# Windowed attention and a gated feed-forward on one core: whole loads per batch and kind, stores of 32 or 64 rows, and a new order

## The chip, the cores and the metric

One core of one Trainium2 chip runs the whole program. The metric is the device time of one execution, in microseconds (us); three executions of the kernel before gave 328.67, 329.82 and 332.52 us, median 329.82 us.

## The reference, cut to what matters

Shapes: 8 batches, 8 heads, 576 tokens, 64 features a head; the model width is 512, the hidden width 1024.

```python
mask_plain = (rel >= 0) & (rel < 32)                        # heads 0 to 3
mask_dil   = (rel >= 0) & (rel < 128) & (rel % 4 == 0)      # heads 4 to 7
attn = softmax(where(mask, q @ k.T / 8, -1e9))
x = (attn @ v)                                              # [batch, token, 512]
for b in range(8):
    scores = x[b] @ w_gate                                  # one gate score per token
    top = the 128 tokens of highest score
    ye = relu(x[b, top] @ w1) @ w2
    out[b, top] = x[b, top] + sigmoid(scores[top])[:, None] * ye
```

All other rows of `out` are `x`. All inputs and the output are float32.

## The kernel before, in words

**Attention units.** Each batch is cut into five units `u`. Units 0 and 1 take the dilated heads ("kind 1"), two of the four residues of the token number each; units 2 and 3 take the plain heads ("kind 0"), 256 tokens each; unit 4 takes the last 64 tokens of both kinds. A unit's steps are `scores` (S: 8 mask products L327 and up to 64 score products L335 into the PSUM tile `s`), `maximum` (MX), `subtract` (SU, both VectorE), `turn` (TR, 4 transposes), `exps` (EX, ScalarE), `attend` (V: 64 products with the values L370 into the PSUM tile `a`), `divisors` (DN), `divide` on VectorE (XM, L392) or on ScalarE (XA, L390, eight instructions), `store` (ST). `s` and `a` have one buffer each.

**Loads.** `load_qk` (LQ, L255 to 283) loads what one unit needs of queries and keys into one of four buffers `qk`; `load_v` (LV, L288 to 302) loads a unit's values into one of four buffers `v` (or `vl` for unit 4). Runs are 1024 and 1152 bytes for queries and keys of units 0 to 3, 192 to 384 bytes in unit 4, 2080 or 4160 bytes for values. They take 2560 KB and 2145 KB a batch. All are issued by SyncE (SP), whose instructions run in order, so that a DMA which waits (for a buffer, or for the rows it stores) holds up every one behind it.

**Stores.** `store` (L394 to 408) writes a unit's 128 x 512 tile `x` to the output in runs of 1024 bytes. For units 0 to 3 it issues two DMAs of 128 rows and 128 KB each, one for each half `e` of the tile:

```python
dst = o[0:4*P, 256:512].rearrange("(e n r) f -> e r n f", e=2, r=DIL)      # units 0 and 1
nc.sync.dma_start(out=dst[1 - e, 2*u:2*u + 2], in_=x[:, e])                # outermost size of out: r = 2
dst = o[...].rearrange("(c e q) f -> c q e f", e=2, q=G)                   # units 2 and 3
nc.sync.dma_start(out=dst[:, :, e], in_=x[:, e])                           # outermost size of out: c = 4
```

Unit 4 has three smaller DMAs (L405: 32 rows, L408: 16 rows twice) whose output has an outermost size of 32 and 16.

**Routing and feed-forward.** Gate sums per token: GM and GA (GpSimd, then ScalarE) or GD (VectorE); RO, SC, SP and SB bring them in order of the tokens and make a row of them; RK, RC and RA rank them; MK (GpSimd) and MV (VectorE) mark, one token block an instruction (L490), which token has which rank; PK picks the indices (PE), GT gathers the 128 rows (GpSimd DMA). The weights (LW, 16 DMAs of 256 KB through four buffers `raw`) are split once into two parts (WH or WV, and WL on GpSimd). XT, XH and XL turn and split the gathered rows; N (one batch) or F (a pair of batches) is the first product, Y the second, YO the sum and SY the scatter (GpSimd DMA). Pairs are set by the GROUP lines: 0, 1, (2, 3), (4, 5), (6, 7).

**Order.** The order of all steps over all engines is written out by hand in the string ORDER (L42 to 111); each engine takes its own instructions in that order. Nine idle products on a zero tile (L660) run ahead of it.

Of the kernel before, what the change touches and what calls it, by code (L numbers as in the profile page):

```python
# [8 lines left out]
F32 = mybir.dt.float32  # L9
F32R = mybir.dt.float32r  # L10
BF16 = mybir.dt.bfloat16
# [8 lines left out]
P = 128  # L20
# [8 lines left out]
QW, KW = 256, 288  # L29
LQ, LK = 128, 48  # L30
# [6 lines left out]
BUFS = dict(qk=4, v=4, s=1, dt=2, pt=2, a=1, x=5, gm=2, m=4, xe=4, h=1, raw=4, oh=1, sb=1, rm=1, xh=1, xl=1, hh=1, hl=1, mx=3, den=3, rin=3, rx=2, g=8, ix=8, junka=1, junkv=1)  # L37
# [6 lines left out]
GROUP 1 1  # L44
GROUP 2 2 3
GROUP 3 4 5
GROUP 4 6 7
LQ 0 0, C 1, C 5, LQ 0 1, LW 0, LQ 0 2, LV 0 0, C 6, LQ 0 3, S 0 0, C 2, MX 0 0, SU 0 0, LV 0 1, WH 0, S 0 1, WL 0,
LW 1, C 3, TR 0 0, MX 0 1, LW 2, EX 0 0, SU 0 1, LQ 0 4, V 0 0, S 0 2, DN 0 0, LW 3, XA 0 0, TR 0 1, MX 0 2, LV 0 2,
LW 4, SU 0 2, LQ 1 0, TR 0 2, LV 0 3, WV 1, S 0 3, C 4, EX 0 1, EX 0 2, ST 0 0, V 0 1, MX 0 3, WH 2, SU 0 3, LQ 1 1,  # L50
WH 3, DN 0 1, S 0 4, XM 0 1, LV 0 4, TR 0 3, MX 0 4, GM 0 0, V 0 2, EX 0 3, SU 0 4, ST 0 1, GD 0 1, TR 0 4, WL 3,
LQ 1 2, GA 0 0, S 1 0, LV 1 0, DN 0 2, EX 0 4, WL 1, RX 0, WV 4, XA 0 2, LW 5, MX 1 0, LQ 1 3, WL 2, SU 1 0, TR 1 0,
WL 4, LW 6, S 1 1, ST 0 2, GM 0 2, V 0 3, MX 1 1, LW 7, LW 8, EX 1 0, DN 0 3, XM 0 3, GA 0 2, LV 1 1, SU 1 1, V 0 4,
GM 0 3, ST 0 3, S 1 2, DN 0 4, XM 0 4, LQ 1 4, GA 0 3, TR 1 1, MX 1 2, GM 0 4, V 1 0, EX 1 1, SU 1 2, ST 0 4, DN 1 0,
S 1 3, GA 0 4, WV 5, WL 5, TR 1 2, XA 1 0, MX 1 3, LV 1 2, RO 0, LV 1 3, SU 1 3, LQ 2 0, SC 0, TR 1 3, SP 0, LW 9,
EX 1 2, V 1 1, GM 1 0, ST 1 0, SB 0, DN 1 1, LQ 2 1, EX 1 3, RK 0 0, S 1 4, XA 1 1, RK 0 1, LV 1 4, RK 0 2, LQ 2 2,
# [12 lines left out]
GM 2 4, MV 1 3, TR 3 2, MV 1 4, ST 2 4, V 3 0, GA 2 4, S 3 3, DN 3 0, LV 3 4, XM 3 0, PK 1, EX 3 2, MX 3 3, GM 3 0,
ST 3 0, RO 2, SG 1, SU 3 3, HT 0 1, LQ 4 2, SH 1, GA 3 0, V 3 1, IX 1, SC 2, GT 1, LV 4 0, HI 0 1, S 3 4, DN 3 1,  # L70
LV 4 1, XA 3 1, HO 0 1, TR 3 3, MX 3 4, LQ 4 3, SP 2, Y 0 2, SU 3 4, LV 4 4, Y 0 3, EX 3 3, GD 3 1, V 3 2, SB 2,
ST 3 1, S 4 0, RX 3, DN 3 2, XM 3 2, LV 4 2, TR 3 4, MX 4 0, LQ 4 4, GM 3 2, XT 1, EX 3 4, Y 0 4, SU 4 0, XH 1,
Y 0 5, RK 2 0, GA 3 2, ST 3 2, TR 4 0, RK 2 1, V 3 3, RK 2 2, S 4 1, EX 4 0, LV 4 3, DN 3 3, XM 3 3, Y 0 6, LQ 5 0,
MX 4 1, GM 3 3, Y 0 7, ST 3 3, SU 4 1, V 3 4, RK 2 3, GA 3 3, S 4 2, RK 2 4, LV 5 4, DN 3 4, XL 1, XA 3 4, TR 4 1,
MX 4 2, LQ 5 1, RC 2, N 1 0 0, RA 2, SU 4 2, MK 2 0, N 1 0 1, MV 2 4, MK 2 1, TR 4 2, YO 0, EX 4 1, ST 3 4, MK 2 2,
V 4 0, GD 3 4, MK 2 3, S 5 0, EX 4 2, LV 5 0, SY 0, DN 4 0, PK 2, XM 4 0, LQ 5 2, MX 5 0, RO 3, GM 4 0, SG 2, ST 4 0,
SU 5 0, N 1 0 2, SH 2, TR 5 0, GA 4 0, IX 2, SC 3, GT 2, S 4 3, V 4 1, MX 4 3, LQ 5 3, SP 3, EX 5 0, SU 4 3, LV 5 1,
N 1 0 3, SB 3, DN 4 1, TR 4 3, XA 4 1, RK 3 0, N 1 1 0, N 1 1 1, RK 3 1, N 1 1 2, RK 3 2, N 1 1 3, RK 3 3, RL 1 0,
ST 4 1, GD 4 1, S 4 4, RL 1 1, RK 3 4, V 4 2, LQ 5 4, MX 4 4, RC 3, EX 4 3, SU 4 4, HT 1 0, DN 4 2, HT 1 1, HI 1 0,
RA 3, LV 5 2, TR 4 4, MV 3 0, MK 3 3, XA 4 2, MV 3 1, XT 2, MV 3 2, MK 3 4, S 5 1, RX 4, HO 1 0, PK 3, MX 5 1,  # L80
LQ 6 0, SU 5 1, XH 2, V 4 3, GM 4 2, ST 4 2, SG 3, IX 3, XL 2, HI 1 1, S 5 2, LV 5 3, EX 4 4, GT 3, DN 4 3, TR 5 1,
SH 3, LQ 6 1, XA 4 3, MX 5 2, Y 1 0, SU 5 2, Y 1 1, HO 1 1, TR 5 2, Y 1 2, GA 4 2, GM 4 3, ST 4 3, V 4 4, S 5 3,
DN 4 4, EX 5 1, LV 6 4, XM 4 4, GA 4 3, XT 3, MX 5 3, ST 4 4, V 5 0, XH 3, SU 5 3, Y 1 3, EX 5 2, DN 5 0, LQ 6 2,
GD 4 4, XA 5 0, TR 5 3, LV 6 1, Y 1 4, XL 3, RO 4, Y 1 5, SC 4, GD 5 0, ST 5 0, V 5 1, S 5 4, EX 5 3, LV 6 2, DN 5 1,
XM 5 1, SP 4, LQ 6 3, MX 5 4, GM 5 1, Y 1 6, SB 4, ST 5 1, SU 5 4, Y 1 7, RK 4 0, GA 5 1, TR 5 4, V 5 2, RK 4 1,
S 6 0, EX 5 4, LV 6 0, DN 5 2, RK 4 2, XA 5 2, F 2 0 0, LQ 6 4, MX 6 0, F 2 0 1, SU 6 0, F 2 0 2, RK 4 3, RK 4 4,
TR 6 0, RX 5, YO 1, GM 5 2, ST 5 2, V 5 3, S 6 1, DN 5 3, EX 6 0, LV 6 3, SY 1, XA 5 3, RC 4, MX 6 1, LQ 7 0,
F 2 0 3, RA 4, SU 6 1, MK 4 3, F 2 1 0, MV 4 0, MV 4 1, TR 6 1, MV 4 2, GA 5 2, F 2 1 1, ST 5 3, GD 5 3, V 5 4,
HH 2 0, MV 4 4, S 6 2, HL 2 0, EX 6 1, LV 7 4, DN 5 4, PK 4, XM 5 4, LQ 7 1, F 2 1 2, SG 4, MX 6 2, ST 5 4, F 2 1 3,
SU 6 2, F 2 2 0, HH 2 1, GD 5 4, TR 6 2, V 6 0, SH 4, IX 4, HL 2 1, GT 4, S 6 3, EX 6 2, LV 7 0, DN 6 0, RO 5,  # L90
XA 6 0, MX 6 3, LQ 7 2, SU 6 3, F 2 2 1, SC 5, TR 6 3, SP 5, F 2 2 2, GD 6 0, ST 6 0, SB 5, V 6 1, RK 5 0, S 6 4,
EX 6 3, LV 7 1, DN 6 1, F 2 2 3, RK 5 1, LQ 7 3, XA 6 1, MX 6 4, F 2 3 0, SU 6 4, F 2 3 1, RK 5 2, F 2 3 2, HH 2 2,
# [22 lines left out]
def tile_window_attention_moe(ctx, tc, qt, kt, va, vb, w_gate, w1, w2, masks, mask_l, ident, slots, toks, outs, capacity):  # L115
# [647 lines left out]
```

## Time and profile before

| | |
|---|---|
| median of three executions | 329.82 us |
| the profiled execution's own time | 329.4 us |
| its span, first to last instruction | 327.5 us |
| mean granted TensorE clock | 0.84 of full speed |
| PE busy | 247.0 us (75%) |
| VectorE, ScalarE, GpSimd busy | 154.5, 113.9, 94.5 us |
| moved by DMA | 57.86 MB |

How to read it: the engines run beside each other, each in its own order, so their busy times don't add up. The profiled execution lasts 1.9 us longer than its span; that is outside the first and the last instruction. The DMA share is the mean over 16 DMA engines: 0.125 can be two of them always busy or all of them an eighth of the time. Where queues overlap it can pass 1 a little.

### The profile page before, as it was taken

The numbers are of one execution on the slowest core, as the hardware profiler recorded it, in microseconds if no ns is written. First come the engines' busy times: TensorE is split into PE (matmuls) and PEld (weight loads), VectorE is DVE, ScalarE is ACT, GpSimd is POOL, SyncE is SP. The second block draws the span as 40 slices with busy tenths as digits, with TensorE's granted clock in tenths as the row PEclk, the third lists the DMA queues.
The fourth block names the chain that finished last, engine by engine and source line by source line (L and its number), as shares of the span: only waits on it lengthen the run. The fifth ranks groups of instructions, "written<-read, shape, count | busy, mean of one in ns | idle before, by whom it ended". The sixth has DMA issues, their size and how long they took to land.

```text
span 327.5 us, 14421 instructions
## 1 busy us (share of the span) xinstructions
PE 247.0 (75%) x6345; PEld 206.5 (63%) x6345; DVE 154.5 (47%) x437; ACT 113.9 (35%) x383; POOL 94.5 (29%) x122
## 2 busy tenths in 40 slices
PE   5665455376769289772099859879978999999993
PEld 2554345264656178661088748769866889989982
DVE  5346234525458246572027737765944662630310
ACT  1325136333343525240015724434524665200200
POOL 7258023634154122134010501201122454130111
PEclk9555559656599769799559999999979999999998
DMA  6967586776696478676775596557755614101001
GB/s 189 292 157 275 158 268 170 249 228 207 174 275 220 141 217 270 218 212 183 231 237 157 152 298 181 176 159 228 215 177 155 191 67 127 49 20 47 32 7 59
DMA packets 55454, 57.86 MB, mean 177 GB/s; under 512 B 18656, under 2 KB 46432, under 8 KB 55392
## 3 DMA queue, kind: packets, MB, share of 16 engines
q1 hardware_dynamic: 53824, 52.65, 53.7%
q0 software_dynamic: 1280, 4.20, 3.8%
q8 instruction: 50, 0.82, 1.1%
q10 hardware_dynamic: 288, 0.10, 0.1%
q14 instruction: 12, 0.10, 0.1%
HBM read 45.39 MB, written 11.53 MB: 174 GB/s over the span
## 4 chain that ended last, share of the span: by engine, by line
PE 42%; DMA 27%; issue 17%; SPq 7%; POOL 2%; DVE 2%; ACT 1%; POOLq 0%
DMA qk<-in_kt_dram 10%; PE py L617 7%; PE a L370 7%; PE s L335 7%; PE ph L574 6%; DMA out_dram<-x 6%; SPq L264 5%; PE t L354 4%; DMA vl<-in_va_dram 3%; DMA raw<-in_w_dram 3%; PE pi L498 2%; PE ph L591 2%; DMA qk<-in_qt_dram 2%; DMA wg<-in_gate_dram 2%; PE s L327 1%
## 5 line engine op out<-in xcount | busy, mean ns | idle before, releaser
L335 PE MATMUL s<-qk 64*32 64x64 f32 (+1 forms) x2432 | 40.7, 252 | 46.3 <-DMA qk<-in_kt_dram 40.4
L335 PEld LDWEIGHTS s<-qk 64*32 64x32 f32 (+1 forms) x2432 | 33.5, 119 | 50.8 <-DMA qk<-in_kt_dram 21.3
L420 POOL TENSOR_TENSOR gm<-x,wg 128x512 f32<-128x512 f32 x28 | 35.9, 1284 | 83.1 <-DVE x L392 53.7
L341 DVE TENSOR_REDUCE mx<-s 128x8 f32<-128x512 f32 x40 | 27.5, 688 | 63.2 <-PE s L335 63.2
L359 ACT ACTIVATE pt<-t 128x512 f32<-128x512 f32 x40 | 24.0, 600 | 78.6 <-PE a L370 57.2
L370 PE MATMUL a<-v,pt 64*32 64x65 f32 x2048 | 31.5, 248 | 12.4 <-DMA v<-in_va_dram 7.7
L390 ACT ACTIVATE x<-a,rin 128x64 f32<-128x64 f32 x168 | 36.7, 336 | 9.9 <-PE a L370 5.3
L370 PEld LDWEIGHTS a<-v,pt 64*32 64x32 f32 x2048 | 25.2, 116 | 18.9 <-issue 15.1
L354 PE MATMUL t<-id,dt 128*128 128x128 f32 x160 | 31.9, 334 | 2.6 <-DVE dt L346 2.6
L574 PE MATMUL ph<-xh,w1h 128*128 128x256 f32 x96 | 28.2, 294 | 0.1
L346 DVE TENSOR_TENSOR dt<-s,mx 128x512 f32<-128x512 f32 x40 | 27.6, 690 | 1.2
L617 PE MATMUL py<-w2h,hh 128*128 128x512 f32 x64 | 28.1, 440 | 0.0
L354 PEld LDWEIGHTS t<-id,dt 128*128 128x128 f32 x160 | 22.6, 169 | 8.4 <-DVE dt L346 3.0
L574 PE MATMUL ph<-xl,w1h 128*128 128x256 f32 x96 | 27.0, 281 | 0.4 <-issue 0.4
L430 ACT ACTIVATE junk<-gm 128x256 bf16<-128x256 f32 x56 | 23.5, 420 | 10.7 <-POOL gm L420 9.7
L574 PE MATMUL ph<-xh,w1l 128*128 128x256 f32 x96 | 26.9, 281 | 0.0
L380 DVE TENSOR_SCALAR den<-a 128x8 f32<-128x8 f32 x40 | 6.6, 164 | 43.0 <-PE a L370 42.8
L617 PE MATMUL py<-w2l,hh 128*128 128x512 f32 x64 | 26.0, 406 | 0.0
L617 PE MATMUL py<-w2h,hl 128*128 128x512 f32 x64 | 26.0, 406 | 0.0
L470 DVE SCALAR_TENSOR_TENSOR rm<-sb,ts,thr 128x576 bf16<-128x576 f32 (+4 forms) x40 | 23.7, 635 | 2.2 <-ACT sb L462 2.2
L490 POOL TENSOR_SCALAR oh<-slots_sb,rk 128x128 f32<-128x128 f32 (+1 forms) x17 | 11.0, 652 | 40.6 <-DVE rk L484 40.6
L518 POOL DMA_INDIRECT xe<-out_dram,ix x8 | 8.5, 1064 | 42.2 <-DVE ix L502 19.9
(100 smaller groups left out, 415.1 us busy)
## 6 DMA issues: line engine op xcount, KB each, us to landing
v<-in_va_dram SPq DMA_DIRECT2D x16, 520.0 KB
out_dram<-x SPq DMA_DIRECT2D x64, 128.0 KB
qk<-in_qt_dram SPq DMA_DIRECT2D x31, 256.0 KB
qk<-in_kt_dram SPq DMA_DIRECT2D x23, 288.0 KB
v<-in_va_dram SPq DMA_DIRECT2D x16, 260.0 KB
raw<-in_w_dram SPq DMA_DIRECT2D x16, 256.0 KB
qk<-in_kt_dram SPq DMA_DIRECT2D x24, 96.0 KB
v<-in_va_dram SPq DMA_DIRECT2D x16, 130.0 KB
```

Source lines behind the costliest of these rows:

```text
L335: nc.tensor.matmul(st[G * a:G * a + m, h, i * GK + lo:i * GK + hi], q[r, hh, q0:q0 + m], k[r, hh, k0 + lo:k0 + hi], start=False, stop=i == 3)
L341: nc.vector.tensor_reduce(out=mx, in_=st[:, :, 0:4 * GK].rearrange("p u (i k) -> p u i k", i=4), axis=AX.X, op=ALU.max)
L346: nc.vector.tensor_tensor(out=dt.rearrange("p (u h) (e k) -> p u (h e) k", u=2, e=2), in0=st[:, :, 0:4 * GK].rearrange("p u (i k) -> p u i ...
L354: nc.tensor.transpose(tt[:, i * P:(i + 1) * P], dt[:, i, :], id32)
L359: nc.scalar.activation(pt.rearrange("p i q -> p (i q)"), tt, AF.Exp, scale=SCALE)
L370: nc.tensor.matmul(av[G * a:G * (a + 1), e, f], pt[r, i, G * a:G * (a + 1)], v[r, values(u, e, a), f], start=True, stop=True)
L390: nc.scalar.activation(xv[:, e, i], av[:, e, i, 0:D], AF.Copy, scale=rin[:, e, i:i + 1])
L420: nc.gpsimd.tensor_tensor(out=gm, in0=X["x", b, u], in1=gate_w(u).unsqueeze(1).to_broadcast([P, 2, 256]), op=ALU.mult)
L430: nc.scalar.activation(junk, X["gm", b, u][:, c], AF.Copy, scale=UP, accum_out=acc)
L470: nc.vector.scalar_tensor_tensor(out=X["rm", b][:, t, 0:n], in0=X["sb", b][:, t * P:S], scalar=ts[:, b, t, 1:2], in1=thr[:, 0:n], op0=ALU. ...
L574: nc.tensor.matmul(out, WS1[w][:, i, f * P:(f + 1) * P], X["x" + x, e][:, i, :], start=i == 0 and n == 0, stop=i == 3 and n == 2)
L617: nc.tensor.matmul(X["py", b], X["h" + x, e][:, i, j * P:(j + 1) * P], WS2[w][:, i, :], start=i == 0 and k == 0, stop=i == 7 and k == 2)
```

## The change

- **Loads.** `load_qk` now loads one kind of one batch whole: 128 x 2 x 576 float32, 576 KB, in one DMA with runs of 4608 bytes (in two parts for the kind 1 of batch 0). Tiles: `q1`, `k1` with two buffers, `q0`, `k0` with one. The three key loads of batch 0 are issued by ScalarE. `load_v` has three parts a batch: `v1` (dilated, 780 KB in two DMAs), `v0` (plain and last block, 1170 KB in one), both with one buffer, and `vl` (195 KB in two). Queries and keys are 2304 KB a batch, values 2145 KB as before. SP and ScalarE issue 216 such loads and stores in place of 288, 50.5 MB in place of 52.6 MB.
- **Stores.** Units 0 and 1: two DMAs of 64 rows (128 KB). Units 2 and 3: four DMAs of 32 rows (64 KB). Their output has an outermost size of 64 and 32.
- **Places.** `attend` writes the half of the dilated units that belongs to the first tokens first, so that `x` and the gate sums stand in order of the token halves.
- **Marks.** One VectorE instruction for all five blocks of a batch (three batches), or five on GpSimd (five batches), in place of 23 and 17 single ones. The fifth block is padded to 128 rows everywhere; `rm` is one tile, filled with zeros once (GpSimd).
- **Divides.** 27 on VectorE and 13 on ScalarE in place of 19 and 21.
- **Idle products.** 51 products on the zero tile, 128 x 128 by 512 columns, in 14 groups of 1 to 7, stand in ORDER among the steps of batches 0 to 2.
- **Order.** A new ORDER; the pairs are 0, (1, 2), (3, 4), (5, 6), 7. In each batch the two dilated units come first, then units 4, 2 and 3.

```diff
-BUFS = dict(qk=4, v=4, s=1, dt=2, pt=2, a=1, ...)
+BUFS = dict(q1=2, k1=2, q0=1, k0=1, v0=1, v1=1, s=1, a=1, ..., dt=2, pt=2, ...)
+    def load_qk(which, b, kind, part=None):
+        src = (qt if which == "q" else kt)[b, kind].rearrange("p (h s) -> p h s", h=2)
+        if (which, b, kind) not in X:
+            X[which, b, kind] = new(f"{which}{kind}", [P, 2, S], f"{which}{b}_{kind}")
+        n = 256 if which == "q" else 2 * SR
+        lo, hi = (0, S) if part is None else (0, n) if part == 0 else (n, S)
+        (nc.scalar if which == "k" and b == 0 else nc.sync).dma_start(out=X[which, b, kind][:, :, lo:hi], in_=src[:, :, lo:hi])
+    def load_v(b, part):
...
+        elif part == 1:
+            X["v", b, 0] = v = new("v0", [P, 9, VW], f"vp{b}")
+            nc.sync.dma_start(out=flat(v), in_=va[b, :, 4 * VW:13 * VW])
+        else:
+            X["v", b, 1] = v = new("v1", [P, 8, VW], f"vd{b}")
+            nc.sync.dma_start(out=flat(v[:, 0:4]), in_=va[b, :, 0:4 * VW])
+            nc.sync.dma_start(out=flat(v[0:HB, 4:8]), in_=va[b, G:G + HB, 0:4 * VW])
@@ store
-            dst = o[0:4 * P, 256:512].rearrange("(e n r) f -> e r n f", e=2, r=DIL)
-            for e in range(2):
-                nc.sync.dma_start(out=dst[1 - e, 2 * u:2 * u + 2], in_=x[:, e])
+            dst = o[0:4 * P, 256:512].rearrange("(e n r) f -> r n e f", e=2, r=DIL)
+            for r in range(2):
+                nc.sync.dma_start(out=dst[2 * u + r], in_=x[HB * r:HB * (r + 1)])
...
-            for e in range(2):
-                nc.sync.dma_start(out=dst[:, :, e], in_=x[:, e])
+            for c in range(4):
+                nc.sync.dma_start(out=dst[c], in_=x[G * c:G * (c + 1)])
@@ attend
-                    nc.tensor.matmul(av[G * a:G * (a + 1), e, f], ...
+                    nc.tensor.matmul(av[G * a:G * (a + 1), 1 - e if u < 2 else e, f], ...
@@ mark
+        if eng is nc.vector:
+            eng.tensor_tensor(out=oh, in0=row.unsqueeze(1).to_broadcast([P, NTOK, P]),
+                              in1=rk[:, b].unsqueeze(2).to_broadcast([P, NTOK, P]), op=ALU.is_equal)
+        else:
+            for t in range(NTOK):
+                eng.tensor_scalar(out=oh[:, t], in0=row, scalar1=rk[:, b, t:t + 1], scalar2=None, op0=ALU.is_equal)
+    def idle(n):
+        pw = bank(f"pw_{len(idles)}")
+        idles.append(pw)
+        for _ in range(n):
+            nc.tensor.matmul(pw, warm[:, 0:P], warm, start=True, stop=True)
```

Where the plain tiles of the next batch are loaded, in the new ORDER (batch 0 to 1; K and Q are loads of keys and queries, VL of values, S the scores, V the products with the values):

```
S 0 4, C 4, XM 0 2, TR 0 1, K 1 0, MX 0 4, Q 1 0, ..., S 1 0, ..., S 1 1, ..., V 0 4, W 2, Q 2 1, ..., S 1 4, XM 0 4,
VL 1 1, TR 1 1, ..., V 1 0, ..., V 1 1, ..., V 1 4
```

## Rows read from the trace of the kernel before

**Rows 1.** The page: span, busy time of PE, and the tenths over 40 slices of 8.2 us each (PE busy, granted clock, DMA share, GB/s).
```profile
span 327.5 us, 14421 instructions
...
PE   5665455376769289772099859879978999999993
...
PEclk9555559656599769799559999999979999999998
DMA  6967586776696478676775596557755614101001
```

**Rows 2.** Busy time of each engine in five stretches that make up the span (start:end, length, busy us and instructions of PE, PE's weight loads, VectorE, ScalarE, GpSimd; granted clock, DMA share, GB/s), and in the first 280 us.
```profile
0.00:117.50 117.50, 71.41 (x2377) 55.23 (x2377) 53.88 (x140) 41.77 (x136) 47.53 (x75) 0.68 0.72 217
117.50:180.00 62.50, 45.20 (x1224) 37.65 (x1224) 29.14 (x90) 19.08 (x63) 12.84 (x13) 0.81 0.71 212
180.00:277.00 97.00, 85.31 (x2460) 74.14 (x2459) 57.35 (x175) 46.16 (x169) 26.89 (x26) 0.98 0.59 177
277.00:322.50 45.50, 45.12 (x290) 39.47 (x288) 13.53 (x34) 6.91 (x15) 6.33 (x7) 1.00 0.11 38
322.50:327.50 5.00, 0.00 (x0) 0.00 (x0) 0.55 (x1) 0.00 (x0) 0.97 (x1) 0.77 0.14 52
...
0.00:280.00 280.00, 204.91 (x6081) 169.86 (x6081) 142.32 (x406) 108.60 (x372) 88.19 (x115) 0.82 0.67 201
```

**Rows 3.** Who waited for whom, PE's waits for loads (engine, line, releaser: us in total, times, longest).
```profile
PE s L335 <- DMA qk<-in_kt_dram: 40.4, 13, 13.7
...
PEld s L335 <- DMA qk<-in_qt_dram: 18.8, 5, 6.9
...
PE a L370 <- DMA v<-in_va_dram: 7.7, 4, 2.9
```

**Rows 4.** The chain of work that ended last, from 25 to 49 us (start, us, what).
```profile
25.80 9.86 DMA out_dram<-x
...
35.73 2.51 SPq L264
...
38.28 6.67 DMA qk<-in_kt_dram
...
45.09 1.38 PE s L335 x53
46.47 1.04 PE t L354 x4
47.51 1.14 PE a L370 x64
```

**Rows 5.** Stretches by what the DMA engines move, columns as in rows 2. First two with loads alone or nearly, then four in which stores of units 0 and 1 are left alone, one with stores of units 2 and 3 (L403), one with the end of these and the stores of unit 4 (L405, L408).
```profile
9.00:15.00 6.00, 3.34 (x164) 2.80 (x152) 1.75 (x4) 0.97 (x3) 1.28 (x1) 0.50 1.05 311
25.00:29.00 4.00, 2.50 (x78) 1.71 (x76) 3.36 (x10) 2.02 (x6) 3.23 (x3) 0.50 1.02 367
35.50:38.50 3.00, 1.29 (x95) 1.32 (x99) 0.08 (x1) 0.00 (x0) 0.00 (x0) 0.50 0.14 51
107.00:109.00 2.00, 1.45 (x74) 0.99 (x72) 0.59 (x6) 0.37 (x1) 0.00 (x0) 1.00 0.13 49
...
265.50:267.00 1.50, 1.50 (x8) 1.23 (x7) 0.92 (x5) 1.03 (x6) 0.33 (x1) 1.00 0.13 48
268.50:270.00 1.50, 1.50 (x71) 1.27 (x70) 0.66 (x3) 0.51 (x3) 1.48 (x3) 1.00 0.14 49
271.50:274.50 3.00, 3.00 (x82) 2.90 (x82) 0.53 (x3) 1.69 (x9) 1.64 (x2) 1.00 0.27 89
274.50:278.00 3.50, 3.50 (x29) 3.35 (x29) 0.32 (x2) 2.26 (x11) 1.92 (x2) 1.00 0.65 183
```

**Rows 6.** SP's own instructions from 259 to 275 us: the last eight stores of units 0 to 3 (start, us, engine, line, operation, count).
```profile
259.40 7.74 SPq L399 DMA_DIRECT2D out_dram<-x  x4
267.24 7.03 SPq L403 DMA_DIRECT2D out_dram<-x  x4
```

**Rows 7.** The page's DMA queues and issues: the queue of SP (packets, MB, share of 16 engines) and the stores (line, engine, operation, count, KB each).
```profile
q1 hardware_dynamic: 53824, 52.65, 53.7%
...
out_dram<-x SPq DMA_DIRECT2D x64, 128.0 KB
```

**Rows 8.** Groups of instructions that the change touches (line, engine, operation, tiles, shapes, count | busy us, mean ns of one | idle before).
```profile
L390 ACT ACTIVATE x<-a,rin 128x64 f32<-128x64 f32 x168 | 36.7, 336 | 9.9 <-PE a L370 5.3 <-DVE rin L381 4.5
...
L392 DVE TENSOR_TENSOR x<-a,rin 128x512 f32<-128x512 f32 x19 | 13.1, 692 | 1.4 <-POOL oh L490 0.3
...
L490 POOL TENSOR_SCALAR oh<-slots_sb,rk 128x128 f32<-128x128 f32 (+1 forms) x17 | 11.0, 652 | 40.6 <-DVE rk L484 40.6
...
L490 DVE TENSOR_SCALAR oh<-slots_sb,rk 128x128 f32<-128x128 f32 (+1 forms) x23 | 6.9, 346 | 0.4
...
L660 PE MATMUL pw<-warm 128*128 128x512 bf16 x9 | 3.6, 585 | 1.2 <-DVE warm L160 1.2
...
L207 POOL MEMSET thr<- 128x576 f32 x1 | 0.6, 579 | 0.0
```

More of the change, by code (lines that the diff above doesn't have):

```diff
@@ L28 @@
 NU = 5
-QW, KW = 256, 288
-LQ, LK = 128, 48
+LK = 48
 VW = 4 * (D + 1)
@@ L52 @@
[L52 to L56, printed above, removed]
@@ L304, in values @@
-    def values(u, e, a):
-        if u < 2:
-            return a // 2 + (2 if e == 0 and a % 2 == 0 else 0)
-        return a if u < 4 or a < 3 else 0
+        return 1, 512 + 16 * r, SR * r, 0, LK, 16
+    def load_qk(which, b, kind, part=None):
[5 more added lines that the diff above has]
+        (nc.scalar if which == "k" and b == 0 else nc.sync).dma_start(out=X[which, b, kind][:, :, lo:hi], in_=src[:, :, lo:hi])
@@ new lines, in load_v, with flat @@
+    def load_v(b, part):
+        def flat(v):
+            return v.rearrange("k a f -> k (a f)")
+        if part == 2:
+            X["v", b, 2] = v = vls[b % 2]
+            for h in range(2):
+                nc.sync.dma_start(out=flat(v[HB * h:HB * h + LK]), in_=vb[b, LK * h:LK * (h + 1)])
+        elif part == 1:
[5 more added lines that the diff above has]
+            nc.sync.dma_start(out=flat(v[0:HB, 4:8]), in_=va[b, G:G + HB, 0:4 * VW])
@@ L312, in scores, with values @@
+    def values(b, u, e, a):
+        if u < 2:
+            return X["v", b, 1][:, 2 * u + a // 2 + (4 if e == 0 and a % 2 == 0 else 0)]
+        if u < 4:
+            return X["v", b, 0][:, 4 * (u - 2) + a]
+        return X["v", b, 2][:, a - 1] if a in (1, 2) else X["v", b, 0][:, 8]
     def scores(b, u):
-        t = X.pop(("qk", b, u))
-        nq = LQ if u == 4 else QW
-        q = t[:, 0:2 * nq].rearrange("p (h n) -> p h n", h=2)
-        k = t[:, 2 * nq:2 * nq + 2 * KW].rearrange("p (h n) -> p h n", h=2)
@@ L628, in scatter @@
                                      in_=X.pop(("y", b))[:m], in_offset=None)
+    def idle(n):
[3 more added lines that the diff above has]
+            nc.tensor.matmul(pw, warm[:, 0:P], warm, start=True, stop=True)
+    idles = []
     do = dict(
-        LQ=load_qk, LV=load_v, C=constants, S=scores, MX=maximum, SU=subtract, TR=turn, EX=exps,
+        Q=lambda *a: load_qk("q", *a), K=lambda *a: load_qk("k", *a), VL=load_v, C=constants, W=idle, S=scores, MX=maximum, SU=subtract, TR=turn, EX=exps,
         V=attend, DN=divisors, XM=lambda b, u: divide(b, u, False), XA=lambda b, u: divide(b, u, True), ST=store,
@@ L657, in tile_window_attention_moe @@
     nc.scalar.activation(tab, warm[:, 0:1], AF.Exp)
-    pw = bank("pw")
-    for _ in range(WARM):
-        nc.tensor.matmul(pw, warm[:, 0:P], warm, start=True, stop=True)
+    idle(WARM)
     route = "GM GA GD RX RO SC SP SB RK RC RA MK MV PK IX SG SH GT LW WH WV WL XT XH XL F HH HL N RL HT HI HO Y YO SY".split()
```

252 lines of the change are left out of this document (102 added, 150 removed).

## The prediction

> **What bounds the kernel now.** I read the page first, then the waits, the chain, the table of stretches, and SP's own instructions. On the page PE is busy three quarters of the span, the clock row lies at 5 or 6 in most of the first third, and the DMA row stands between 4 and 9 until slice 32 and is nearly empty behind it [rows 1]. That looks like a kernel in which nothing is full. The stretches show where PE's idle time lies: 46.1 of 117.5 us in the first, 17.3 of 62.5 in the second, 11.7 of 97 in the third, 0.4 of 45.5 in the last [rows 2]. The waits say on what: scores on keys, 40.4 us in 13 waits, weight loads of scores on queries, 18.8 us, products on values, 7.7 us [rows 3]. So loads are late although the DMA share is 0.67 over 280 us.
>
> The chain says why: its loads stand behind stores. A store of unit size takes 9.86 us to land, SP's next query load is stuck 2.51 us in its issue, its key load lands 6.67 us after it, and only then do scores run [rows 4]. The share while stores are alone decides it. Loads reach a share of 1.02 to 1.05 and 311 to 367 GB/s; in four stretches far apart in which only stores of units 0 and 1 are left the share is 0.13 to 0.14 at 48 to 51 GB/s, and with stores of units 2 and 3 it is 0.27 at 89 GB/s [rows 5]. 0.14 x 16 is 2.2 engines, 0.27 x 16 is 4.3: those stores run on two and on four of the 16 DMA engines, at the outermost sizes of their output, 2 and 4. [...]
>
> I check that this is a bound. 128 KB at 48 GB/s are 2.73 us, times 32 are 87 us; at 89 GB/s 1.47 us, times 32 are 47 us. If the four share the same two engines, these two carry stores for 134 us. The other 44.3 of 52.65 MB [rows 7] are loads spread over all: at 311 GB/s 142 us on every engine. The sum is 277 us for the two busiest, and the DMAs of SP end near 278 us: two engines never rest while fourteen wait for them. Before 277 us this kernel is bound by two DMA engines, behind it by PE.
>
> **The change part by part.**
>
> *Stores.* The output's outermost size becomes 64 and 32. The nearest rows are the stores of unit 4 with 32 and 16: the stretch that holds them, still mixed with the others' end, has a share of 0.65 and 183 GB/s [rows 5], well over what four engines give. I take them as spread over 16. Then 8.4 MB cost 27 us on all engines in place of 134 us on two. [...]
>
> [...]
>
> *Loads.* 216 issues in place of 288, 50.5 in place of 52.6 MB: 2.1 MB, 7 us at 311 GB/s. Runs grow to 4608 bytes; I take the rate of the loads-only row, 311, with 367 as the upper end and the first stretch's present mean of 217 as the lower. All at 311 is 162 us, so the queue as a whole is below PE's work.
>
> *The first stretch* ends where batch 0's first feed-forward product runs: until then PE has only units and routing, and DMA is ahead of it in need. In the new order 87 issues with 23.3 MB stand ahead of that product (22.6 MB in the old one, which took 117.5 us). At 311 GB/s that is 75 us, and 2 us until the first bytes land; for waits on buffers I add 5 us: 82 us. Ends: 65 us (at 367) and 107 us (at 217).
>
> *Idle products.* 51 at 3.6 us / 9 = 0.40 us [rows 8] are 20 us at the low clock, half at the high one, all in this stretch. PE's own work there is 71.4 us at a mean clock of 0.68, so 49 us at full clock. Together 59 us with a high clock, 91 us if nothing changes. The cover is DMA's 82 us; at the low end of the clock 9 us stand out. Nine idle products ran first and the clock stood near 0.9 in slice 1 and at 0.5 in the next slices, in which PE worked half of the time [rows 1]; with shorter waits I expect it up most of the time, and cost them at nothing.
>
> *The rest is PE's.* 45.2 + 85.3 + 45.1 = 175.6 us stand behind 117.5 us [rows 2]; scaled by the granted clock 165 us; I take 171 us. Pairs and singles are as many as before, three and two. Of the 45.5 us at the end 0.4 are idle, and I keep that. For the 126 us ahead of them I take 8% idle, between none and the third stretch's 12%: 137 us. Together 182.5 us (ends 165 and 194). Behind PE's last product come y, the scatter and the end, 5.0 us as now.
>
> *Single buffers.* q0, k0, v0 and v1 can be loaded only when the last user is done. Next batch's k0 and q0 (1.18 MB) go out behind the last plain scores, and two dilated units stand between that and their first use; v0 (1.20 MB) goes out behind the last plain products, with two dilated products ahead. Each is 3.8 us at 311 GB/s and a landing of a few us, against two units that now take 14 us (280 / 40 each). Queued behind a waiting load on SP are stores, and behind these a gather; the 8% hold this.
>
> *Small edits.* Marks: 25 x 0.652 = 16.3 us of GpSimd in place of 11.0, and VectorE 3 x some 0.9 us (an estimate: 640 elements a row, at 692 ns for 512) in place of 6.9 us. Eight divides move: ScalarE -8 x 8 x 0.336 = -21.5 us, VectorE +8 x 0.692 = +5.5 us. `rm` filled once: 0.58 us for 576 float32, so 1.3 to 2.6 us of GpSimd by bytes or elements, behind other constants. Fifth block padded: five products a batch longer, under 0.1 us each. Key loads of batch 0 on ScalarE's queue: three issues of 0.6 us ahead of its first exponential. All [rows 8], all on engines that are at 30 to 60% [rows 2], so nothing; without that cover the gain and loss here is about 5 us either way. Gate sums at their places change one column index.
>
> **Sum.** 82 + 182.5 + 5 = 269.5 us of span, 271.4 us with the 1.9 us around it; the profiled execution's 329.4 us is 0.4 us under the median of 329.82 us. I predict 271 us.
>
> **The rivals.**
> 1. *Stores at half width.* If a store from 32 or 64 rows reaches 8 engines' worth, at 48 / 2.2 = 22 GB/s an engine, a unit's 256 KB takes 1.49 us in place of 0.84. In the first stretch lie ten such units: 6.5 us; behind it PE hides them. 278 us. The share of 0.65 in the unit 4 row speaks neither way.
> 2. *Single buffers show.* If 3 us at each of seven turns of plain tiles stay open: 21 us, 292 us. For it: 2.38 MB must come in one turn. Against: two units of cover.
> 3. *The stores don't spread* (the change doesn't do what it says). Then the two engines carry 134 + 42.1 MB / 311 GB/s = 135, so 270 us, and the 49 us from 278 us to the end stay: 320 us. Against: the unit 4 row.
> 4. *Slower than before.* The single buffers turn loading and computing into alternation: k0, q0 and v0 at 7.7 us and a landing of 6.67 us [rows 4] are 14.4 us a turn; if PE has only one unit of 3.5 us to do meanwhile (scores, turn, products, [rows 4]), 11 us x 7 = 77 us, 348 us. It decides from 8.4 us a turn on (59 us / 7). Against: in the order two dilated units and feed-forward pieces stand in each turn.
>
> **How the numbers follow.** Forecast 0.70, rival 1 0.10, rival 2 0.08, rival 3 0.08, rival 4 0.04. A measurement of this kernel tells about 1% from no change. Rival 3 could come out within 1% in a quarter of its cases: faster 0.94, same 0.02, slower 0.04. The forecast's own ends, all terms at one end at once, are 65 + 165 + 7 = 237 and 107 + 194 + 7 = 308 us. Terms don't all fall together: I cut to 250 to 297 us, which holds rivals 1 and 2 and leaves out 3 and 4 and the far ends.
>
> **What would show it.** Right: with stores alone in flight the share is no longer near 0.14; SP's four-store issues fall from 7 us to 2 or 3; the first feed-forward product of batch 0 starts near 82 us; scores wait for keys for under 20 us in all; PE is over 90% busy from there to 5 us before the end. Wrong: stores alone at 0.14 (rival 3), or waits of 5 us and more at the scores of each batch's first plain unit behind a plain key load (rivals 2 and 4), or PE full but at half clock in the first stretch, where the idle products would then cost their time.

## The result, and the profile after

The kernel after takes 308.0 us (median of four executions, 305.36 to 310.9), the kernel before 331.17 us beside it: a ratio of 0.930 [0.917, 0.943]. The change helps by 7%; 271 us were predicted, with 297 us as the upper end, so the time lies 11 us outside the range. Medians count every execution, ratios with an interval only those within 1.5% of their kernel's fastest; the profiled execution, 310.9 us, is the longest of the four and lies outside that.

The page after, with the rows that answer to [rows 1] and, of the queues, that of the instructions; the last line is the chain of work by engine:

```profile
span 309.2 us, 14324 instructions
...
PE 255.7 (83%) x6396; PEld 208.2 (67%) x6396; DVE 158.1 (51%) x426; ACT 100.3 (32%) x318; POOL 102.1 (33%) x131
...
PE   7577649786889868888895868979989999999993
...
PEclk9759968897859987987996958997989999999999
DMA  6995788987879686579365865285427312020000
...
q8 instruction: 50, 0.82, 1.1%
...
PE 62%; issue 28%; DMA 4%; DVE 2%; POOL 2%; ACT 1%; POOLq 0%; ACTq 0%
```

The same line of the kernel before:

```profile
PE 42%; DMA 27%; issue 17%; SPq 7%; POOL 2%; DVE 2%; ACT 1%; POOLq 0%
```

DMA falls from 27% to 4% of the chain that sets the end, so the load waits are gone as foretold. "Issue" rises from 17% to 28%: time in which the engine of the chain waits for nothing that the profile names. Pauses of up to 0.15 us between instructions make 1.2 us of it; the waits of PE alone follow below. The stretches, cut at the first product of batch 0's feed-forward (91.8 us) and at PE's last (columns as in [rows 2]):

```profile
0.00:91.80 91.80, 66.51 (x2035) 45.66 (x2035) 47.53 (x112) 28.57 (x89) 45.02 (x71) 0.80 0.83 261
91.80:304.00 212.20, 189.23 (x4366) 162.55 (x4361) 109.91 (x315) 71.70 (x231) 56.12 (x60) 0.91 0.49 148
304.00:309.20 5.20, 0.00 (x0) 0.00 (x0) 0.70 (x1) 0.00 (x0) 0.97 (x1) 0.88 0.13 50
```

The reader is to hold these against the forecast's 82, 182.5 and 5 us: 9.8 us too much ahead of the cut, 29.7 behind it, and the end as foretold. The waits, to be read beside [rows 3]:

```profile
PEld a L346 <- issue: 22.9, 24, 3.3
PE a L346 <- issue: 21.0, 12, 4.0
PEld s L311 <- issue: 19.9, 17, 3.4
...
PE s L311 <- issue: 13.6, 14, 2.9
...
PE s L302 <- issue: 4.8, 3, 2.2
...
PE s L311 <- DMA k<-in_kt_dram: 3.5, 2, 3.2
```

PE's waits for keys fell from 40.4 to 3.5 us. Its waits marked issue (the PE lines alone, without those of its weight loads, PEld), summed over all lines of that view, rose from 15.3 us before to 42.1 us. Below, "waits marked issue" is this sum.

What is behind "issue" shows where products stand densely. First the chain, then the table of stretches cut at the starts of those waits:

```profile
27.05 2.07 issue
...
31.65 1.47 issue
...
35.73 1.23 issue
...
39.14 4.04 issue
```

```profile
27.05:31.65 4.60, 2.53 (x127) 1.85 (x127) 2.32 (x6) 1.10 (x2) 2.06 (x11) 1.00 0.28 60
31.65:35.73 4.08, 2.48 (x128) 1.90 (x127) 2.29 (x5) 1.24 (x4) 2.50 (x2) 1.00 0.92 320
35.73:39.14 3.41, 2.18 (x128) 1.77 (x127) 2.06 (x4) 1.00 (x4) 2.24 (x2) 1.00 0.64 156
39.14:53.20 14.06, 10.02 (x254) 6.64 (x254) 5.68 (x16) 3.88 (x14) 6.15 (x6) 0.76 0.84 258
```

From one wait to the next PE runs 128 products and 128 weight loads, 256 instructions (a record or two are missing), and twice that in the last row. The queue of instructions moved 50 packets of 16 KB (0.82 MB), and PE's 12,792 instructions over 50 are 256. So PE's code comes in blocks of 256 instructions, and it waits for the next one: in the rows above it works some 2.2 to 2.5 us and stands 1.2 to 2.1 us, once 4. Counting the trace's single instructions and packets, 29 gaps of PE, at some 50 block ends (40.5 us of its 46.9 us between products), begin at the same place in the count of 256 and end 1.2 to 1.6 us after the packet of the next block has landed; in the kernel before 13 such gaps make 16.4 us of 74.
One block by this count: PE begins it at 29.11 us, the next block's packet starts at 30.39 us and lands at 31.77 us, PE has run the block by 31.65 us and goes on at 33.12 us. So the next block is there 4.0 us after PE began this one, whose work took 2.5 us; PE stands idle for the difference.

### The profile page after: what moved, and what is told of

The parts are those of the page before. It is cut to its first block, busy times and chain, and to the rows that moved or that the text cites. A ratio compares the mean times of both kernels' runs of the same rounds, so it can differ in the third digit from the quotient of the medians.

```text
span 309.2 us, 14324 instructions
## 1 busy us (share of the span) xinstructions
PE 255.7 (83%) x6396; PEld 208.2 (67%) x6396; DVE 158.1 (51%) x426; ACT 100.3 (32%) x318; POOL 102.1 (33%) x131
## 4 chain that ended last, share of the span: by engine, by line
PE 62%; issue 28%; DMA 4%; DVE 2%; POOL 2%; ACT 1%; POOLq 0%; ACTq 0%
PE a L346 11%; PE s L311 10%; PE ph L546 9%; PE t L330 8%; PE py L589 6%; PE pw L607 4%; PE s L302 3%; DMA k<-in_kt_dram 2%; PE pi L470 2%; PE ph L563 2%; PE pr L420 1%; PE pa L430 1%; DMA q<-in_qt_dram 1%; PE pr L418 1%; PE px L525 1%
## 5 line engine op out<-in xcount | busy, mean ns | idle before, releaser
L335 ACT ACTIVATE pt<-t 128x512 f32<-128x512 f32 x40 | 23.8, 600 | 100.9 <-PE t L330 72.5
L311 PE MATMUL s<-k,q 64*32 64x64 f32 (+2 forms) x2432 | 40.0, 241 | 17.2 <-issue 13.6
L311 PEld LDWEIGHTS s<-k,q 64*32 64x32 f32 (+1 forms) x2432 | 33.7, 115 | 20.0 <-issue 19.9
L346 PE MATMUL a<-vp,pt 64*32 64x65 f32 x1280 | 24.1, 242 | 10.5 <-issue 10.5
L546 PE MATMUL ph<-xh,w1h 128*128 128x256 f32 x96 | 30.2, 315 | 1.4 <-issue 1.4
L366 ACT ACTIVATE x<-a,rin 128x64 f32<-128x64 f32 x104 | 22.8, 332 | 19.5 <-DVE rin L357 7.1
L464 POOL TENSOR_SCALAR oh<-slots_sb,rk 128x128 f32<-128x128 f32 x25 | 15.0, 613 | 36.4 <-DVE rk L454 34.6
L346 PEld LDWEIGHTS a<-vp,pt 64*32 64x32 f32 x1280 | 18.8, 114 | 12.0 <-issue 10.4
L442 DVE SCALAR_TENSOR_TENSOR rm<-sb,ts,thr 128x576 bf16<-128x576 f32 (+3 forms) x32 | 25.3, 838 | 2.4 <-ACT sb L435 2.4
L403 ACT ACTIVATE junk<-gm 128x256 bf16<-128x256 f32 x56 | 23.3, 416 | 10.0 <-POOL gm L393 9.1
L599 POOL DMA_INDIRECT out_dram<-y,ix x8 | 8.0, 998 | 53.8 <-DVE y L594 53.8
L330 PEld LDWEIGHTS t<-id,dt 128*128 128x128 f32 x160 | 20.6, 161 | 6.4 <-issue 2.8
```

What stands on the lines that cost most here:

```text
L311: nc.tensor.matmul(st[G * a:G * a + m, h, i * GK + lo:i * GK + hi], q[r, hh, q0:q0 + m], k[r, hh, k0 + lo:k0 + hi], start=False, stop=i == 3)
L330: nc.tensor.transpose(tt[:, i * P:(i + 1) * P], dt[:, i, :], id32)
L335: nc.scalar.activation(pt.rearrange("p i q -> p (i q)"), tt, AF.Exp, scale=SCALE)
L346: nc.tensor.matmul(av[G * a:G * (a + 1), 1 - e if u < 2 else e, f], pt[r, i, G * a:G * (a + 1)], values(b, u, e, a)[r, f], start=True, sto ...
L366: nc.scalar.activation(xv[:, e, i], av[:, e, i, 0:D], AF.Copy, scale=rin[:, e, i:i + 1])
L403: nc.scalar.activation(junk, X["gm", b, u][:, c], AF.Copy, scale=UP, accum_out=acc)
```

## The experiments

Each was run with the kernel before beside it (medians 330.3 to 333.2 us).

**1. The parts of the change.** The kernel before with stores that spread alone:

```diff
-    for e in range(2):
-        nc.sync.dma_start(out=dst[1 - e, 2 * u:2 * u + 2], in_=x[:, e])
+    for e in range(2):
+        for r in range(2):
+            nc.sync.dma_start(out=dst[1 - e, 2 * u + r], in_=x[HB * r:HB * (r + 1), e])
...
+    for c in range(4):                                   # units 2 and 3
+        nc.sync.dma_start(out=dst[c], in_=x[G * c:G * (c + 1)])
```

> The kernel before, with its loads and its order untouched; only the stores of units 0 to 3 are cut so that each covers 64 or 32 rows (four DMAs of 64 KB a unit). Theory P (two busy DMA engines bound the kernel before; freed of them, PE waits at block ends for its own instructions, which come over the same DMA engines): waits of scores on keys fall from 40 us to under 10, the time falls to 300 to 315 us, most of the whole change's gain. Rival L (the whole loads made the gain, the stores little): 322 us or more, and scores still wait 30 us for keys.

319.24 us, 0.947 [0.939, 0.955], between the two expectations; its PE still waits for keys:

```profile
PE s L335 <- DMA qk<-in_kt_dram: 26.6, 11, 12.3
```

And the kernel after with the old stores:

```diff
-    for r in range(2):
-        nc.sync.dma_start(out=dst[2 * u + r], in_=x[HB * r:HB * (r + 1)])
+    for e in range(2):
+        nc.sync.dma_start(out=dst[e, 2 * u:2 * u + 2], in_=x[:, e])
```

> The kernel after with the old cut of the stores (two DMAs of 128 rows a unit, outermost size of the output 2 and 4). Theory P: the two engines carry 134 + 135 us again, and batch after batch waits for its loads: 320 to 335 us. Rival L: the whole loads keep the gain, 305 to 312 us.

319.93 us, 0.958 [0.951, 0.965], at the edge of theory P. Stores alone give 5%, everything else alone 4%, together 7%. With the stores alone PE's waits for keys stay at 26.6 of 40.4 us, so the stores were not all that made keys late. With the old stores PE waits 10.2 us for loads, in place of 3.5 us, and its waits marked issue are already 41 us. With both halves those are what remains.

**2. What makes the block late: loads.** Loads in shorter runs (queries, keys and values cut into runs of about 1 KB):

```diff
+        for lo, hi in ([(0, 288), (288, S)] if part is None else [(lo, hi)]):
```

> The kernel after with the same bytes loaded in runs of 1040 to 1152 bytes in place of 4160 to 9360 (two or four DMAs in place of one or two). Theory P1 (a block of PE's instructions waits on its DMA engine behind a number of data packets, so long packets make it late): PE's waits for nothing that the profile shows fall by a third or more against the kernel after, the clock rises, 290 to 302 us. Theory P2 (it waits behind the bytes that are queued, whatever their cut): 304 to 312 us, those waits unchanged.

308.33 us, waits marked issue 43.2 us, as theory P2 had it: the length of the packets ahead is not it. Loads left out, from batch 1 on and from batch 3 on:

```diff
+        if b > 0:          # the second kernel: b > 2
+            X[which, b, kind] = X[which, 0, kind]
+            return
```

> The kernel after without the loads of queries, keys and values of batches 1 to 7, which read the tiles of batch 0 instead (37 MB less; weights, stores and gathers stay). Theory P: with the DMA engines nearly free the blocks of PE's instructions come early, PE's waits for nothing that the profile shows fall to under a third, the granted clock rises to 0.95 or more and the time falls to 260 to 280 us. Rival O (the new order's own dependences between the engines make PE wait, and the clock falls with that): those waits stay, since PE waits for loads in hardly 4 us of the kernel after: 298 us or more.

> The kernel after without the loads of queries, keys and values of batches 3 to 7, which read the tiles of batch 2. Up to the first feed-forward product (92 us in the kernel after, 74 us without all loads of batches 1 to 7) nothing is taken away. Theory P (blocks of PE's instructions come late behind loads, and each wait at a block's end also lets the clock fall): 287 to 294 us, the first feed-forward product still at 89 to 94 us. Rival F (the 34 us of the run without loads came from the DMA-bound start alone): 300 us or more.

273.58 us, 0.820 [0.813, 0.828], and 287.78 us, 0.871 [0.866, 0.878]. PE's two largest waits and the clock row of the first:

```profile
PE s L318 <- issue: 11.4, 11, 1.7
PE a L353 <- issue: 6.3, 8, 1.5
```

```profile
PEclk9888899998999989999999999799999999999997
```

Both times lie where theory P had them. The waits marked issue halve without loads, to 22.4 us, where under a third was expected: PE stops at block ends without loads too, but shorter; without the late loads they are 35.1 us. Counted from the trace, from the moment PE begins a block, the next block's packet starts after 1.7 us (median) in the kernel after and more than 3 us later at 12 of 49 blocks; without late loads after 1.3 us, and at 6 of 48; without loads after 1.2 us, and at 1 of 46. So loads make the late packets more frequent. Pacing the loads from batch 2 on, so that each large one is issued only when the last but one has landed:

```diff
+            nc.sync.dma_start(out=pacer[:, n:n + 1], in_=sent[-2])   # waits for the load before the last
         nc.sync.dma_start(out=out, in_=in_)
```

> The kernel after with loads of batches 1 to 7 paced: before each of them SP copies 4 bytes of the tile loaded two loads before, so that at most two loads of 0.5 to 0.7 MB are in flight (v0 goes in two parts). Same bytes. Theory P2 (a block of PE's instructions waits behind the bytes that stand in the DMA queues): PE's waits for nothing that the profile shows fall from 42 us to under 30, time 295 to 303 us. Rival P3 (the wait comes from the traffic as such, not from the queue's depth): those waits stay; with SP held up 308 to 320 us.

312.87 us, waits marked issue 45 us, and by the same count a packet delay of 1.9 us, with 14 of 49 over 3 us; with the shorter runs 2.0 us and 16 of 49. So the blocks come late with the traffic, and neither shorter packets nor fewer loads under way changed that. By what way stays open.

**3. The idle products.**

```diff
     def idle(n):
+        if idles:
+            return
```

> The kernel after without the 51 idle products of its order (the nine ahead of it stay). Theory P: they fill time in which PE would wait for loads or for its next block, so the time stays within 4 us of the kernel after (304 to 312 us) while the clock of the first 90 us falls from 0.8 to 0.65 or less. Rival W (they take PE's time and 102 places in its instruction stream): 298 to 304 us. Rival C (they hold the clock up, which the units need): 312 us or more.

306.69 us, 0.920 [0.911, 0.928]. In the first third the clock row now stands mostly at 5 to 7 tenths of full speed (mean of the first 92 us 0.67, in the kernel after 0.80), and the time doesn't move:

```profile
PEclk9555575765799759869996797999999999999999
```

That they cost and bring nothing can't be concluded, though: their removal also takes 102 instructions out and moves later block ends, which by experiment 5 can be worth more than the difference looked for.

**4. Instructions or work.** Two kernels with other scores. In the first, one product with twice the columns serves two heads, in the second the products of every second head get two columns:

```diff
-            nc.tensor.matmul(st[..., i * GK + lo:i * GK + hi], q[r, hh, q0:q0 + m], k[r, hh, k0 + lo:k0 + hi], ...)
+            nc.tensor.matmul(both[:, e, :, lo:hi], q[r, 0, q0:q0 + m], k[r, :, k0 + lo:k0 + hi], ...)
```

```diff
+            hi = lo + 2 if hh else hi
```

> Changed: the two heads of a pair share one score product of twice the columns with the first head's queries as weights, so the second head's scores are others; the keys' columns that go through PE are as many as in the kernel after, the score products and their weight loads half as many: 1216 products and 1216 weight loads fewer, some 2430 instructions of 12,800, which is 9 or 10 blocks of 256 of the 50. Theory B (after this change PE's idle time is the wait at the end of each block of instructions, some 1.4 us each at some 29 of them, and the clock that these gaps cost): 9 or 10 blocks fewer, and in the stretches where they stall, so 7 to 10 stalls fewer, 10 to 14 us of idle time and some of the clock: PE's waits marked issue fall from 42 to about 28 us, 286 to 297 us. Theory W (PE's time follows the columns that go through it; the waits marked issue are a way of the profile to show that): the same columns, 303 to 311 us, waits marked issue near 40 us.

> Changed: the score products of the second head of each pair take 2 key columns and not 64, so most of that head's scores are left out; products, weight loads and their order are those of the kernel after, the columns of the score products are half as many. Theory B: a block of 256 instructions is used up sooner, and PE then waits the longer for the next; the columns saved (in the stretch from 27.05 to 39.14 us of the kernel after, 381 products took 7.19 us of busy time, 19 ns each, so at most 1216 x 19 = 23 us by that row, and about half of it where the other costs of a product stay) go mostly into longer waits: waits marked issue rise from 42 to 46 to 56 us, 300 to 309 us. Theory W: the columns saved come off the time, waits marked issue stay at 42 us or fall: 285 to 297 us.

281.61 us (277.95 to 286.0) and 311.49 us (304.68 to 316.12). The first kernel's page rows and PE's waits:

```profile
span 276.2 us, 11892 instructions
...
PE 239.5 (87%) x5180; PEld 192.4 (70%) x5180; DVE 158.2 (57%) x426; ACT 99.9 (36%) x318; POOL 102.1 (37%) x131
...
q8 instruction: 41, 0.67, 1.0%
```

```profile
PE s L311 <- issue: 9.9, 9, 3.1
PE a L346 <- issue: 6.2, 9, 1.9
```

and the second's:

```profile
PE s L312 <- issue: 17.6, 20, 2.6
...
PE a L347 <- issue: 14.5, 8, 3.9
```

As many columns with nine packets of instructions fewer save 26.4 us; half the columns with as many instructions save nothing. Theory W falls twice. B's estimate was short: of the 33 us between the two profiled spans (the longest execution of the one, the shortest of the other) 19 are waits marked issue (42.1 to 23) and 16 are busy time of PE. Part of the latter is the score products' own, by their groups in the kernel after, the first and the second kernel:

```profile
L311 PE MATMUL s<-k,q 64*32 64x64 f32 (+2 forms) x2432 | 40.0, 241 | 17.2 <-issue 13.6
```

```profile
L311 PE MATMUL s<-k,q 64*32 64x128 f32 (+2 forms) x1216 | 32.3, 286 | 13.5 <-issue 9.9
```

```profile
L312 PE MATMUL s<-k,q 64*32 64x2 f32 (+4 forms) x2432 | 37.1, 210 | 20.7 <-issue 17.6
```

So 7.7 of the 16 us are score products: half as many cost 32.3 us of PE in place of 40.0, half their columns 37.1. So here these products cost more by their number than by their columns, at block ends and in themselves. The other 8 or 9 us come with a higher clock (0.877 to 0.93). B expected the waits to rise with thin products, to 46 us or more, and 300 to 309 us; they stayed at 40 us, and the time is 2.5 us above.

**5. Where the block ends fall.** 32, 64, 96 or 128 short products, behind the first group of idle products, ahead of a gap of 3.22 us in which PE, by the trace of the kernel after, waits for keys (the expectation below names VectorE); nothing else changes:

```diff
+        if len(idles) == 2:
+            for _ in range(32):                          # 64, 96, 128
+                nc.tensor.matmul(pw[0:G, 0:8], warm[:, 0:G], warm[:, 0:8], start=True, stop=True)
```

> Kernel after with 32 short products (32 x 128 by 8 columns, 64 instructions) behind the first group of idle products, where PE waits for VectorE: every later block end falls 64 instructions earlier in the order. (2): the stalls fall on other places, the waits marked issue move from 42 us by 4 us or more and the time with them by 1.5 to 4% either way: 295 to 303 or 313 to 321 us. Rival (the places average out over 50 blocks): 306 to 311 us, waits marked issue 39 to 45 us.

> Kernel after with 64 short products (128 instructions) at the same place: every later block end falls half a block earlier. (2): 295 to 303 or 313 to 321 us, and another time than with 64 instructions. Rival: 306 to 312 us, waits marked issue 39 to 45 us.

> Kernel after with 96 short products (192 instructions) at the same place, every later block end three quarters of a block earlier. (2) Places of the block ends: another time than the kernel after, 308 to 325 us, no sign foretold. Rival (extra instructions cost by their number or by the late start): more than with 128, 326 to 331 us.

> Kernel after with 128 short products (256 instructions, 3.5 us of PE in a gap of some 3 us). (2): the block ends stand where they stood in the kernel after, so its time comes back but for the extra products and one more block end: 309 to 315 us, below the kernels with 64 and 128. Rival: above the kernel with 128 extra instructions, 326 to 335 us.

| extra instructions | median us | to the kernel before |
|---|---|---|
| 0 | 308.0 | 0.930 [0.917, 0.943] |
| 64 | 323.8 | 0.969 [0.947, 0.991] |
| 128 | 325.7 | 0.980 [0.958, 1.001] |
| 192 | 309.6 | 0.934 [0.927, 0.941] |
| 256 | 310.0 | 0.921 [0.912, 0.931] |

The extra products take 0.96 us (32) to 3.58 us (128). A quarter or half a block costs 16 to 18 us by the medians and 13 to 17 us by the ratios, three quarters or a whole block, with more extra work, 2 us by the medians and nothing clear of the noise by the ratios. The first two lie above what (2) expected, the last two inside it. Nor is it the late start: the scores behind that gap begin at 11.87 us in the kernel after, at 13.45, 12.46, 11.96 and 14.69 us in the four. By the count of 256 the gaps still begin at that one place: 40.6 of 44.6 us with 192 extra instructions, 40.7 of 46.1 us with 256. By this, what costs is where in the order the block ends fall. With 128 extra instructions two waits carry it, 48.6 of 55.4 us marked issue:

```profile
PE a L346 <- issue: 29.0, 15, 4.5
PE s L311 <- issue: 19.6, 12, 5.1
```

With 64 the sum is only 43.6 us, so there my expectation of the waits failed; of the 13.5 us by which that profiled span is longer 8.9 us are busy time of PE (264.6 us at a clock of 0.846), and what lowers the clock there isn't settled.

**6. Fewer instructions, whole computation.** Masks merged by products over several query groups, with constants that VectorE builds; masks added by products on the full array, with the mask rows loaded behind the first keys; the same without idle products; and both with the mask rows loaded first, by GpSimd's queue:

```diff
-        for a in range(4):
...
-                nc.tensor.matmul(st[G * a:G * (a + 1), h, 0:4 * GK], id16[r], mk[r, m:m + 4, :], ...)
+        for h in range(2):
+            for lo, hi in ((0, P),) if u < 4 else ((0, HB), (HB, 96), (96, P)):
+                nc.tensor.matmul(st[lo:hi, h, 0:4 * GK], id16[:, lo:hi], mk[:, max(u - 1, 0)], ...)
```

> The kernel after with the mask products of a unit in two products of 128 rows (a stationary tile that picks one of two mask rows for each of the four row groups) in place of eight of 32; unit 4 keeps eight. 192 products and 192 weight loads fewer: 384 of 12,800 places in PE's stream, 1.5 of 50 blocks. Theory P: each block of a dense unit costs about 5 us, so 7 us, and 2 to 6 us of PE's time: 296 to 302 us. Rival O (the stream of instructions does not matter): at most the products' own time, 303 to 307 us.

> The whole computation, with fewer instructions for PE: the mask of a unit is added by 2 products of 128 x 128 by 256 columns (6 for unit 4) in place of 8 on tiles of 64 x 32; the mask rows for the four kinds of unit come from DRAM as a constant of 256 KB in two DMAs, and VectorE no longer builds them. 208 products and 208 weight loads fewer, 416 instructions, 1.6 blocks of 256. Theory B with the price that the kernel with half the score products gave (26.4 us for 9.5 blocks, 2.8 us a block): 4.6 us less than the kernel after, 303 us, between 299 and 306. Rival (the mask products stand where no block is late, or the products on the full array cost what the blocks save): 306 to 311 us, not to be told from the kernel after.

> The whole computation: as the one before, and without the 51 idle products of the stretches behind the first nine; 518 instructions fewer than the kernel after in all, 2.0 blocks. Theory B: 5.7 us less than the kernel after, 302 us, between 298 and 306; the granted clock of the first third falls below 0.75 as it did without the idle products alone, which cost nothing there. Rival (the low clock of the first third costs what the blocks save): 306 to 312 us.

> The whole computation: the full-array mask products as before (416 instructions fewer than the kernel after), but the mask rows of the last three kinds of unit are loaded by GpSimd's queue as its first instruction, not behind the key loads. (1) The late start was the loss: the wait of 6.4 us at the mask rows goes, 302 to 309 us. (2) The places of the block ends are the loss: the time stays near 320 us, 314 to 322.

> The whole computation: as the one before without the 51 idle products, 518 instructions fewer than the kernel after. (1) The wait of 7.8 us goes and the time falls from 309.4 to 300 to 304 us, under the kernel after. (2) No fixed sign: 300 to 315 us.

310.61, 320.78, 309.44, 316.64 and 310.85 us. The first two lie outside all that was expected, the third where its rival had it, the last two where (2) had them. In the second PE waits once for the mask rows:

```profile
PE s L278 <- DMA mk<-in_masks_dram: 6.4, 1, 6.4
```

Without that wait it is 316.64 us (310.93 to 326.21), and the one without idle products gains nothing by the same step. The rest is not at block ends: in the second kernel the waits marked issue are 39.2 us, 2.9 us fewer than in the kernel after. Its mask products take longer, here beside those of the kernel after:

```profile
L302 PE MATMUL s<-mk,id 64*32 64x256 bf16 x320 | 16.2, 311 | 5.5 <-issue 4.8 <-DVE mk L174 0.5
```

```profile
L278 PE MATMUL s<-mk,id 128*128 128x256 bf16 (+2 forms) x112 | 22.1, 302 | 6.6 <-DMA mk<-in_masks_dram 6.4
```

112 products on the full array cost 22.1 us of PE where 320 small ones cost 16.2 us; the products of the first kernel, 128 in its trace, take 21.3 us. For the second kernel the account closes: its profiled span is 10.1 us longer, 6.4 us by the wait for the rows, 6.6 us by PE's busy time, 5.9 of them mask products, less 2.9 us of waits marked issue. So the rival named in its expectation, that products on the full array cost what the blocks save, holds in kind; (1) and (2) of the later kernels both left it out. No version that computes everything beat the kernel after by more than its spread.

## Why the prediction was wrong

- **The two-engine bound: right for the stores, not the whole of it.** The old stores held loads back, but with the stores spread and nothing else changed keys still cost PE 26.6 us in place of 40.4. Four stores of a unit now leave SP in 1.8 us, against 7.03 in [rows 6], and stores of units 2 and 3 alone reach a share of 0.54 where [rows 5] had 0.27. That is 8.6 engines on average, while SP issues one such store every 0.44 us; counted from the trace, 16 packets of stores alone are under way at 242.15 us (units 0 and 1) and at 247.30 us (units 2 and 3), where before it was mostly 2 with stores of units 0 and 1 and 4 with those of units 2 and 3. The 16 engines that the prediction took for the new stores fit that; why 64 and 32 reach them no run shows. Nor does a run show stores alone at the 311 GB/s that the prediction's 27 us take: the second row here has 135 GB/s:

```profile
245.75 1.76 SPq L379 DMA_DIRECT2D out_dram<-x  x4
```

```profile
257.00:257.50 0.50, 0.50 (x4) 0.38 (x3) 0.36 (x2) 0.50 (x3) 0.50 (x1) 1.00 0.54 135
```

- **The step that failed: "The rest is PE's"**, in "For the 126 us ahead of them I take 8% idle" and "scaled by the granted clock 165 us; I take 171 us". 182.5 us became 212.2: 23.0 us idle in place of some 11, and 189.2 us busy in place of 171, at a clock of 0.91. Both terms took it that PE, once loads are early, is idle only for other engines and so runs near full clock. The runs show PE waiting at block ends; half the score products' instructions make the same stretch 193.3 us (77.7 to 271.0), part of it by the products themselves (experiment 4). That block waits lower the clock is shown only in part: in the kernel after the granted clock fell from 1.00 to 0.50 of full speed during three of them (from 39.14, 69.44 and 162.98 us, 3.1 to 4.0 us long), but with 64 extra instructions it is lower (0.846 against 0.877) at about the same sum of waits (43.6 against 42.1 us).
- **The first stretch**, "82 us", took 91.8, by another cause than the working said. Of PE's 25.3 idle us there 3.5 are waits for keys and 19.4 are marked issue. Without the loads of batches 1 to 7 it ends at 74.4 us, with all loads and half the score products at 77.7.
- **Idle products at nothing**: 306.69 us without them bears that out, as far as experiment 5 lets it be told. With them the granted clock of the first 92 us is 0.80, without them 0.67.
- **Single buffers** (rivals 2 and 4): all 3.5 us of waits for keys lie at the first two units of batch 0; no turn of plain tiles shows one. **Rival 1** would have shown as late loads, and doesn't; its 8 engines were a supposition, and the 16 packets at once speak against it. **Rival 3** falls with the stores' share. Its price of 320 us is what the kernel after with the old stores takes (319.93 us), but of that PE waits only 10.2 us for loads and 41 us at waits marked issue, so the match is partly luck.
- **The end** (5.2 us against 5.0) came out as taken. Of the **small edits** ScalarE lost 13.6 us (113.9 to 100.3) and not 21.5: the working multiplied 0.336 us by the count, but by the same row of [rows 8] 168 of these take 36.7 us and not 56.4, since they overlap. As ScalarE was taken at nothing, the sum is not touched.

No rival had the cause. The hint lay in the waits of before: 15.3 us of PE marked issue, 12.1 of it at dense products (L335, L370), that I read as nothing. That they were small because a block arrives while PE waits for keys fits the runs, but wasn't tried by itself: with spread stores alone the waits for keys fell to 26.6 us and these rose only to 16.2.

## What to carry to other kernels

Add up the waits marked issue before forecasting that an engine will be full. Divide its instructions by the packets of its instruction queue, and look whether PE stops every 256 instructions where small products stand densely. On this kernel that time rose from 15.3 to 42.1 us once data was early, and counted in instructions, not in columns: nine packets of instructions fewer took 26.4 us off, half the columns of the score products nothing. On such a kernel an edit of a few per cent can't be judged by itself: shift the block ends by a quarter and a half block and by a whole one, and look what the same work takes. And ask what a product costs before trading many small ones for a few large ones (here 320 took 16.2 us and 112 in their place 22.1).

## What was not expected of the hardware

64 and 128 extra instructions of 1 to 2 us moved a kernel of 308 us by 13 to 18 us, 256 by 2 us or less. Each float32 score product of the code stands as two matmuls and two weight loads in the trace (1216 and 2432), so its instructions weigh double here. DMA traffic delays PE's code: the next block's packet starts over 3 us after PE began a block at 12 of 49 blocks with all loads and at 1 of 46 without, and neither shorter packets (16 of 49) nor fewer loads under way (14 of 49) lowered that.
